# Attention and two feed-forward layers on one core: all products of round 0 with the values in the pair's second step, conversion work moved from the first step to the second

## The chip, the cores and the metric

The kernel runs on one NeuronCore of a Trainium2 chip. The metric is device time in microseconds (us), the median over runs. The engines are PE (TensorE, matrix products and transposes), DVE (VectorE), ACT (ScalarE), POOL (GpSimd) and SP (SyncE, which here issues DMAs). Each works through its own list of instructions in order and waits on semaphores of the others.

## The reference, cut to what matters

```python
scores = scale * np.matmul(q, k.transpose(0, 1, 3, 2))          # 4 x 8 heads, 576 x 576, head size 64
thresh = np.max(scores, axis=-1, keepdims=True) - tau
scores = np.where(scores >= thresh, scores, -1000000000.0)
attn = np.exp(scores - np.max(scores, axis=-1, keepdims=True))
attn = attn / (np.sum(attn, axis=-1, keepdims=True) + 1e-09)
attn_out = np.matmul(attn, v)
...
gate = 1.0 / (1.0 + np.exp(-(x @ w_gate)))                       # x: 2304 x 512, from attn_out
x = gate * (x @ w_val) @ w_out
h = x @ w_in
out = np.where(h >= 1, h, np.where(h <= -1, 0.0, (h + 1) ** 2 / 4)) @ w_out2
```

The change lies in the attention part alone. It alters the order of instructions and no arithmetic.

## The kernel before, in words

The 32 heads are worked as 16 pairs (`NP`), two heads of a pair side by side on the partitions. The 576 query rows of a pair are cut into five steps (`U = 5`): four of 128 rows for both heads, and a fifth that takes the remaining 64 rows of both heads together. The loop `for t in range(N + 9)` counts steps over all pairs, `N = 80`; step `u` of pair `p` is `t = 5 * p + u`. The text calls the steps of a pair first (`u = 0`) to fifth (`u = 4`). The pipeline is written out by hand in this loop: each engine gets its instructions in the order of the calls. In one step there stand, engine by engine:

- PE: `scores` (L252, in the fifth step L248) of this step into the PSUM tiles `wa` (first head) and `wb` (second head); `turns` (L295, L296), the transposes of the masked exponents of two steps ago, into `wt` and `left`; then `attend` (L319), the products with the values, for which the tables `rounds` and `final` say in which step they stand.
- DVE: `maxima` (L261) of this step, one instruction for `wa` and one for `wb`, each closed by a row DVE_READ_ACCUMULATOR that delivers the row's maximum; `masks` (L281) of the step before, one instruction for each head; last the background work.
- ACT: `copies` (L301, L305, L310, L311) of the transposes out of PSUM, `exponents` (L273), and `drain` (L329) of a finished sum `av`.
- POOL: the threshold (L264), a copy of the last 64 columns (L288), the scaling by the reciprocal sums (L350).

There is one `wa` and one `wb`. So `scores` of a step may write `wa` only when `maxima` of the step before has read it, and the same for `wb`; on PE these are two waits, on the first and on the second product of the step.

The products with the values of a pair go in two rounds. Round 0 covers the 256 query rows of the pair's first two steps, round 1 the other 320 rows. Each round is ten products: for both heads four blocks of 128 keys (`c` from 0 to 3) and the rest (`c = 4`, the tile `rl`), summed in the PSUM tile `av`. PE's fp32 products appear as two records each in the trace, so ten products are 20 records. Keys of `rounds` count from the pair's own first step: key 5 is the first step of the next pair, key 6 its second, and so on. Pair 15, the last, goes by `final`.

The background work (`background`, L155 to L169) prepares weights of the first feed-forward layer: one instruction on 128x512 elements at each `next(bg)`. It stands in three of the five steps of a pair, up to `t = 62`; afterwards the same places are "gaps" in which `ffn` puts splits of the attention output (L473, 128x768).

Of the kernel before, what the change touches and what calls it, by code (L numbers as in the profile page):

```python
# [29 lines left out]
def kernel(  # L30
# [169 lines left out]
    def attention():  # L200
# [23 lines left out]
        def load(p):  # L224
            t = qkp.tile([P, 2, S], F32, tag="qk", name="qk")
            nc.sync.dma_start(out=t[:, 0], in_=q[p])
            nc.sync.dma_start(out=t[:, 1], in_=k[p])
            qk[p] = t
# [9 lines left out]
        def corner(p):  # L238
            for e in range(2):
                es = slice(e * R, e * R + R)  # L240
                nc.gpsimd.tensor_copy(corners[p % 2][es, es], qk[p][es, 0, nf * P :])

        def scores(p, u):
            t = qk[p]
            for s in range(2):
                c = slice(s * HS, s * HS + HS)
                if u == nf:
                    nc.tensor.matmul(wa[:, s, :HS], corners[p % 2], t[:, 1, c], start=True, stop=True)  # L248
                    continue
                for e, w in enumerate((wa, wb)):  # L250
                    es = slice(e * D, e * D + D)
                    nc.tensor.matmul(  # L252
                        w[:, s, :HS], t[es, 0, u * P : u * P + P], t[es, 1, c], start=True, stop=True
                    )

        def maxima(p, u):

            t = sp.tile([P, 2, 2, HS], F32, tag="s", name="s")
            mx = mxs[(p * U + u) % 2]
            for e, w in enumerate((wa, wb)[: 1 if u == nf else 2]):  # L260
                nc.vector.tensor_scalar(  # L261
                    t[:, e], w[:, :, :HS], nscale, None, op0=ALU.mult, op1=ALU.min, accum_out=mx[:, 0, e : e + 1]
                )
                nc.gpsimd.tensor_scalar(  # L264
                    mx[:, 1, e : e + 1], mx[:, 0, e : e + 1], tau_b, None, op0=ALU.add
                )
            st[p, u] = t, mx

        def exponents(p, u):
            t, mx = st[p, u]  # L270
            ex = pe_.tile([P, 2, 2, HS], F32, tag="ex", name="ex")
            for e in range(1 if u == nf else 2):
                nc.scalar.activation(ex[:, e], t[:, e], AF.Exp, scale=-1.0, bias=mx[:, 0, e : e + 1])  # L273
            st[p, u] = t, mx, ex

        def masks(p, u):
            t, mx, ex = st.pop((p, u))
            pr = pt[p, u] = pp.tile([P, 2, S], F32, tag="p", name="p")
            for e in range(1 if u == nf else 2):
                c = 2 * nf if u == nf else e * nf + u  # L280
                nc.vector.scalar_tensor_tensor(  # L281
                    pr[:, e], t[:, e].rearrange("p a b -> p (a b)"), mx[:, 1, e : e + 1],
                    ex[:, e].rearrange("p a b -> p (a b)"), op0=ALU.is_le, op1=ALU.mult,
                    accum_out=sums[p % 2][:, c : c + 1],
                )
            lt = lts[p, u] = pp.tile([P, 2, R], F32, tag="lt", name="lt")
            x = pr[:, :, nf * P :] if u < nf else pr[:, :1, nf * P :].broadcast_to((P, 2, R))
            nc.gpsimd.tensor_copy(lt, x)  # L288

        def turns(p, u):  # L290
            pr = pt.pop((p, u))
            for e in range(1 if u == nf else 2):
                for c in range(nf):
                    cs = slice(c * P, c * P + P)
                    nc.tensor.transpose(wt[:, e, cs], pr[:, e, cs], ident)  # L295
            nc.tensor.transpose(left[:, :P], lts.pop((p, u)).rearrange("p a b -> p (a b)"), ident)  # L296

        def copies(p, u):
            r, o = min(u // 2, 1), u % 2 * P if u < nf else 2 * P
            if u < nf:  # L300
                nc.scalar.activation(  # L301
                    rt[r].rearrange("p e c n -> p (e c) n")[:, :, o : o + P],
                    wt.rearrange("p e (c n) -> p (e c) n", n=P), AF.Copy,
                )
                nc.scalar.activation(rl[r][:, o : o + P], left[:, :P], AF.Copy)  # L305
                return
            for e in range(2):
                es = slice(e * R, e * R + R)
                x = wt[:, 0].rearrange("p (c n) -> p c n", n=P)
                nc.scalar.activation(rt[r][:, e, :, o : o + R], x[:, :, es], AF.Copy)  # L310
                nc.scalar.activation(rl[r][es, o : o + R], left[es, es], AF.Copy)  # L311

        def attend(p, r, cs):


            n = NR[r]
            for c in cs:
                for e in range(2):
                    nc.tensor.matmul(  # L319
                        av[e * D : e * D + D, :n], vs[p % 3][:, e, c], rt[r][:, e, c] if c < nf else rl[r],  # L320
                        start=c == 0, stop=c == nf,
                    )
# [5 lines left out]
        def drain(p, r):  # L328
            nc.scalar.activation(x_of(p)[:, r * NR[0] : r * NR[0] + NR[r]], av[:, : NR[r]], AF.Copy)  # L329

        def denom(p):
            rs = sums[p % 2]
            nc.vector.reciprocal(rs, rs)

        def sum_rows(p):

            n = 2 * nf + 1
            nc.scalar.activation(rows[p % 2][:n], left[:n, P : 2 * P], AF.Copy)
            drs[p] = dram.tile([n, P], F32, tag="dr", name="dr")
            nc.sync.dma_start(out=drs[p], in_=rows[p % 2][:n])  # L340
# [7 lines left out]
        def normalise(p, s):  # L348
            x, c = x_of(p), slice(s * HS, s * HS + HS)
            nc.gpsimd.tensor_tensor(x[:, c], x[:, c], rbs[:, p % 2 * S :][:, c], op=ALU.mult)  # L350
# [28 lines left out]
        corner(0)  # L379
        bg = background()  # L380

        rounds = {5: (0, 0, 2), 6: (0, 2, 5), 7: (1, 0, 2), 8: (1, 2, 5)}
        final = {5: (0, 0, 5), 7: (1, 0, 5)}
        parts = {}
        for p in range(NP):
# [2 lines left out]
        for t in range(N + 9):  # L388
            p, u = divmod(t, U)
            on = t < N  # L390
            mk = divmod(t - 1, U) if 1 <= t <= N else None
            at = divmod(t - 2, U) if 2 <= t <= N + 1 else None

            pd, ud = divmod(t - U, U)
            pd2, ud2 = divmod(t - 2 * U, U)
            if ud2 in (2, 3) and 0 <= pd2 < NP:
                normalise(pd2, ud2 - 2)
            if on:
                scores(p, u)
            if t == N + 1:  # L400
                yield t - N, True
            if at:
                turns(*at)
            if ud == 2 and 0 <= pd < NP:
                nc.tensor.transpose(left[: 2 * nf + 1, P : 2 * P], sums[pd % 2], ident)
            for part in parts.get(t, ()):
                attend(*part)
            if on:
                maxima(p, u)
            if at:  # L410
                copies(*at)
            if on:
                exponents(p, u)
            if ud == 1 and 0 <= pd < NP:
                denom(pd)
            if ud == 2 and 0 <= pd < NP:
                sum_rows(pd)
            for part in parts.get(t, ()):
                if part[2][-1] == nf:
                    drain(*part[:2])  # L420
            if mk:
                masks(*mk)
                if mk[1] == nf:
                    nc.gpsimd.tensor_scalar(sums[mk[0] % 2], sums[mk[0] % 2], 1e-9, None, op0=ALU.add)
            if on and u in (0, 2, 3) and t > 2:
                if t <= 12 * U + 2:
                    next(bg, None)
                else:
                    yield t - N, "gap"
            if on:  # L430
                if u == 1 and p + 1 < NP:
                    corner(p + 1)
                if u == 2 and p + 2 < NP:
                    load(p + 2)
                if u == 4 and p + 2 < NP:
                    load_v(p + 2)
                if t == 1 or u == 2 and p % 2 == 0 and p < 12:
                    next(bg, None)
            if ud == 3 and 0 <= pd < NP:
                spread(pd)  # L440
            if t == N - 1:
                wides[:] = [wb, wa, wt]
            if t == N:
                run(bg)
                nc.scalar.activation(dummy, half, AF.Sigmoid)
                st1.close()
            if t == N + 2:
                st2.close()
                ps_o.close()
            yield t - N, False  # L450
# [497 lines left out]
```

## Time and profile before

| | |
|---|---|
| median of 3 runs | 1127.94 us (1127.83 to 1129.14) |
| the profiled execution, its own time | 1128.86 us |
| its span, first to last instruction | 1127.1 us |
| busy in the span | PE 1108.3, DVE 845.5, ACT 621.5, POOL 161.1 us |

Attention fills roughly the first 285 us of the span; the feed-forward layers the rest. Busy time of PE is modelled for pipelined products, so that it is the starts of its rows, and what stands between two of them, that carry an argument. A share of the whole span says little on a change in one stage: what counts there is which engine's instruction is late.

### The profile page before, as it was taken

Reading aid. Unit: us, or ns where it says so; the run is one execution under the profiler, and the core shown is the slowest. Engines: PE = TensorE matmul, PEld = TensorE weight load, DVE = VectorE, ACT = ScalarE, POOL = GpSimd, SP = SyncE. Lnnn points to the kernel's source line nnn. Section 1 sums busy time; section 2 is a strip of 40 time slices with the busy share of each in tenths; the row PEclk is TensorE's granted clock in tenths of the full one; section 3 lists DMA queues with packets and bytes.
Section 4 is the critical chain, followed back from the end, with each engine's and each line's share of the span. In section 5 each row is a group of like instructions: output and inputs, shape, how many; then the busy total and the mean of one; then the engine's idle time right before and its main releaser. Section 6 shows DMA issues by size and latency. Waiting matters only on the chain.

```text
span 1127.1 us, 17344 instructions
## 1 busy us (share of the span) xinstructions
PE 1108.3 (98%) x6372; PEld 946.5 (84%) x6372; DVE 845.5 (75%) x1484; ACT 621.5 (55%) x1048; POOL 161.1 (14%) x315
## 2 busy tenths in 40 slices
PE   8999999999899999999999999989999999999998
PEld 5666666666799999999999999979888888898887
DVE  6999999995899989776687663476767767776663
ACT  6787778886443435333344332365656665666553
POOL 3565666554100000000000000000000000000000
PEclk9999999999899999999999999989999999999999
DMA  4323322313466565555454443033321433243301
GB/s 132 90 77 85 103 87 62 85 52 127 162 203 205 169 213 198 187 167 174 174 184 153 159 153 109 1 112 112 113 106 63 168 113 112 68 156 114 113 19 57
DMA packets 65141, 139.09 MB, mean 123 GB/s; under 512 B 9616, under 2 KB 35872, under 8 KB 65056
## 3 DMA queue, kind: packets, MB, share of 16 engines
q1 hardware_dynamic: 64912, 137.98, 36.7%
q8 instruction: 50, 0.82, 0.3%
q14 instruction: 35, 0.29, 0.1%
q10 hardware_dynamic: 144, 0.00, 0.0%
HBM read 111.15 MB, written 26.81 MB: 122 GB/s over the span
## 4 chain that ended last, share of the span: by engine, by line
PE 91%; DVE 4%; ACT 2%; issue 1%; POOL 0%; DVEq 0%; POOLq 0%; ACTq 0%
PE y L739 15%; PE pu L606 14%; PE y L757 13%; PE pgv L482 8%; PE pgv L481 8%; PE pgv L483 8%; PE av L319 8%; PE w L252 7%; PE w L295 6%; PE w L248 2%; PE left L296 1%; ACT sqs L615 1%; ACT sqs L616 1%; ACT hh L624 1%; PE av L368 0%
## 5 line engine op out<-in xcount | busy, mean ns | idle before, releaser
L481 PE MATMUL pgv<-xflat,win 128*128 128x384 f32 x560 | 188.5, 337 | 5.6 <-ACT act L537 3.8
L739 PE MATMUL y<-wout,hh 128*128 128x512 f32 x576 | 186.0, 398 | 3.0 <-ACT hh L624 3.0
L482 PE MATMUL pgv<-xflat,win 128*128 128x384 f32 x560 | 188.3, 336 | 0.1
L483 PE MATMUL pgv<-xflat,win 128*128 128x384 f32 x560 | 188.2, 336 | 0.0
L757 PE MATMUL y<-hh,wout 128*128 128x512 f32 (+1 forms) x576 | 147.0, 337 | 0.0
L739 PEld LDWEIGHTS y<-wout,hh 128*128 128x128 f32 x576 | 109.4, 190 | 28.1 <-ACT hh L624 3.3
L261 DVE TENSOR_SCALAR_CACHE_REDUCE s<-w,nscale 128x576 f32<-128x576 f32 x144 | 112.7, 817 | 22.5 <-PE w L248 10.7
L541 DVE TENSOR_TENSOR act<-pgv,act 128x384 f32<-128x384 f32 x70 | 38.8, 555 | 105.0 <-PE pgv L483 104.6
L739 PE MATMUL y<-wout,hl 128*128 128x512 f32 x288 | 114.7, 398 | 0.2 <-DVE hl L625 0.2
L481 PEld LDWEIGHTS pgv<-xflat,win 128*128 128x128 f32 x560 | 105.8, 189 | 7.7 <-ACT act L537 4.1
L281 DVE SCALAR_TENSOR_TENSOR p<-s,mx,ex 128x576 f32<-128x576 f32 x144 | 111.7, 809 | 0.5 <-POOL lt L288 0.5
L537 ACT ACTIVATE act<-pgv 128x384 f32<-128x384 f32 x70 | 34.2, 489 | 137.4 <-PE pgv L483 137.2
L273 ACT ACTIVATE ex<-s,mx 128x576 f32<-128x576 f32 x144 | 104.8, 774 | 6.7 <-DVE s L261 6.4
L757 PEld LDWEIGHTS y<-hh,wout 128*128 128x128 f32 x576 | 98.4, 188 | 11.4
L264 POOL TENSOR_SCALAR mx<-mx,tau_b 128x1 f32<-128x1 f32 x144 | 98.1, 685 | 68.3 <-DVE s L261 68.2
L482 PEld LDWEIGHTS pgv<-xflat,win 128*128 128x128 f32 x560 | 106.0, 189 | 2.0 <-DVE xflat L473 0.4
L606 PE MATMUL pu<-xflat,win 128*128 128x384 f32 x576 | 105.1, 337 | 1.0 <-DVE sqs L685 0.7
L483 PEld LDWEIGHTS pgv<-xflat,win 128*128 128x128 f32 x560 | 105.9, 189 | 0.0
L542 ACT ACTIVATE hh<-act 128x384 fp32r<-128x384 f32 x72 | 38.0, 527 | 121.8 <-DVE act L541 121.3
L606 PEld LDWEIGHTS pu<-xflat,win 128*128 128x128 f32 x576 | 100.6, 188 | 2.4 <-DVE sqs L685 1.3
L757 PE MATMUL y<-hl,wout 128*128 128x512 f32 (+1 forms) x288 | 97.3, 338 | 0.0
L301 ACT ACTIVATE r<-w 128x1024 f32<-128x1024 f32 x64 | 65.7, 1026 | 47.7 <-PE w L295 47.7
(140 smaller groups left out, 1918.0 us busy)
## 6 DMA issues: line engine op xcount, KB each, us to landing
wmore<-saved SPq DMA_DIRECT2D x32, 512.0 KB
words<-in_moe_w_out_dram SPq DMA_DIRECT2D x26, 512.0 KB
tsum<-tsaved SPq DMA_DIRECT2D x24, 512.0 KB
wmore<-saved SPq DMA_DIRECT2D x15, 768.0 KB
words<-in_moe_w_in_dram SPq DMA_DIRECT2D x16, 512.0 KB
saved<-w SPq DMA_DIRECT2D x16, 512.0 KB
w<-saved SPq DMA_DIRECT2D x16, 512.0 KB
w<-saved SPq DMA_DIRECT2D x9, 768.0 KB
```

The lines of the kernel that those rows point to most:

```text
L252: nc.tensor.matmul(w[:, s, :HS], t[es, 0, u * P : u * P + P], t[es, 1, c], start=True, stop=True)
L261: nc.vector.tensor_scalar(t[:, e], w[:, :, :HS], nscale, None, op0=ALU.mult, op1=ALU.min, accum_out=mx[:, 0, e : e + 1])
L264: nc.gpsimd.tensor_scalar(mx[:, 1, e : e + 1], mx[:, 0, e : e + 1], tau_b, None, op0=ALU.add)
L273: nc.scalar.activation(ex[:, e], t[:, e], AF.Exp, scale=-1.0, bias=mx[:, 0, e : e + 1])
L281: nc.vector.scalar_tensor_tensor(pr[:, e], t[:, e].rearrange("p a b -> p (a b)"), mx[:, 1, e : e + 1], ex[:, e].rearrange("p a b -> p (a b ...
L319: nc.tensor.matmul(av[e * D : e * D + D, :n], vs[p % 3][:, e, c], rt[r][:, e, c] if c < nf else rl[r], start=c == 0, stop=c == nf,)
L481: nc.tensor.matmul(ps, ih[:, i, kk], xh[:, kk, c], start=(kk == 0), stop=False)
L482: nc.tensor.matmul(ps, ih[:, i, kk], xl[:, kk, c], start=False, stop=False)
L483: nc.tensor.matmul(ps, il[:, i, kk], xh[:, kk, c], start=False, stop=(kk == KD - 1))
L606: nc.tensor.matmul(ps[bank], l[:, k], r[:, k], start=bool(new) and k == m == 0, stop=k == HK - 1 and m == 2, skip_group_check=True,)
L739: nc.tensor.matmul(y[b], l[:, ts_], r, start=first and m == 0, stop=last and m == 2)
L757: nc.tensor.matmul(at(y, a, b), l[:, ds_], r[:, c], start=new and m == 0, stop=last and m == 2, skip_group_check=True,)
```

## The change

```diff
-        rounds = {5: (0, 0, 2), 6: (0, 2, 5), 7: (1, 0, 2), 8: (1, 2, 5)}
+        rounds = {6: (0, 0, 5), 7: (1, 0, 2), 8: (1, 2, 5)}
...
-            if on and u in (0, 2, 3) and t > 2:
+            if on and u in (1, 2, 3) and t > 2:
```

Before, round 0 had its key blocks 0 and 1 (four products) in the first step of the next pair and blocks 2 to 4 (six products) in the second. Now all ten stand in the second step. Round 1 is as before. The background instruction of the first step moves to the second; those of the third and fourth step stay. The instructions on ACT, POOL and SP stand in the same order as before.

PE in the first and second step of a pair, before: `w_126` is `wa`, `w_127` is `wb`, `w_128` is `wt`; the rows begin with the transposes of the first step.

```order
L295 MATMUL w_128<-ident,p 128x128 x8
L296 MATMUL left<-ident,lt 128x128
L319 MATMUL av<-r_160,v_166 64x256 x4
L252 MATMUL w_126<-qk 128x288
L252 MATMUL w_127<-qk 128x288
L252 MATMUL w_126<-qk 128x288
L252 MATMUL w_127<-qk 128x288
L295 MATMUL w_128<-ident,p 128x128 x4
L296 MATMUL left<-ident,lt 128x128
L319 MATMUL av<-r_160,v_166 64x256 x4
L319 MATMUL av<-rl_162,v_166 64x256 x2
L252 MATMUL w_126<-qk 128x288
```

The same place on PE now, from the same transposes on:

```order
L295 MATMUL w_128<-ident,p 128x128 x8
L296 MATMUL left<-ident,lt 128x128
L252 MATMUL w_126<-qk 128x288
L252 MATMUL w_127<-qk 128x288
L252 MATMUL w_126<-qk 128x288
L252 MATMUL w_127<-qk 128x288
L295 MATMUL w_128<-ident,p 128x128 x4
L296 MATMUL left<-ident,lt 128x128
L319 MATMUL av<-r_160,v_166 64x256 x8
L319 MATMUL av<-rl_162,v_166 64x256 x2
L252 MATMUL w_126<-qk 128x288
```

Four products have left the place between the first step's transposes and the second step's scores, and stand before the third step's scores.

DVE over the first and second step of a pair, before, from the first step's maxima on:

```order
L261 TENSOR_SCALAR s,mx_76<-w_126,nscale 128x576
L261 TENSOR_SCALAR s,mx_76<-w_127,nscale 128x576
L281 SCALAR_TENSOR_TENSOR p,sum_81<-s,mx_77,ex 128x576
L165 SCALAR_TENSOR_TENSOR high_84<-raw_87,high_84 128x512
L261 TENSOR_SCALAR s,mx_77<-w_126,nscale 128x576
L261 TENSOR_SCALAR s,mx_77<-w_127,nscale 128x576
L333 RECIPROCAL sum_81<-sum_81 128x9
L281 SCALAR_TENSOR_TENSOR p,sum_80<-s,mx_76,ex 128x576 x2
L261 TENSOR_SCALAR s,mx_76<-w_126,nscale 128x576
```

And now:

```order
L261 TENSOR_SCALAR s,mx_76<-w_126,nscale 128x576
L261 TENSOR_SCALAR s,mx_76<-w_127,nscale 128x576
L281 SCALAR_TENSOR_TENSOR p,sum_81<-s,mx_77,ex 128x576
L261 TENSOR_SCALAR s,mx_77<-w_126,nscale 128x576
L261 TENSOR_SCALAR s,mx_77<-w_127,nscale 128x576
L333 RECIPROCAL sum_81<-sum_81 128x9
L281 SCALAR_TENSOR_TENSOR p,sum_80<-s,mx_76,ex 128x576 x2
L165 SCALAR_TENSOR_TENSOR high_84<-raw_87,high_84 128x512
L261 TENSOR_SCALAR s,mx_76<-w_126,nscale 128x576
```

The conversion (here L165, at every other pair L157) has moved from behind the first step's masks to behind the second step's; both places come after the first step's maxima.

## Rows read from the trace of the kernel before

**Rows 1.** The page: its head, and PE's share from part 1.

```profile
span 1127.1 us, 17344 instructions
...
PE 1108.3 (98%) x6372; PEld 946.5 (84%) x6372; DVE 845.5 (75%) x1484; ACT 621.5 (55%) x1048; POOL 161.1 (14%) x315
```

**Rows 2.** Busy time by stretch: eleven pairs of attention, columns in the first line.

```profile
core 0: us, PE busy (x) PEld busy (x) DVE busy (x) ACT busy (x) POOL busy (x), PEclk, DMA share, GB/s
36.73:218.22 181.49, 181.49 (x1300) 115.24 (x1300) 167.19 (x440) 142.91 (x270) 110.83 (x209) 1.00 0.31 85
```

**Rows 3.** The chain that ended last: start, length, engine, tile, line, records.

```profile
102.72 1.18 PE w L252 x8
...
105.03 1.01 PE av L319 x8
...
107.92 1.45 PE av L319 x12
...
119.22 1.18 PE w L252 x8
...
270.22 2.31 PE av L319 x20
```

**Rows 4.** Timeline of DVE, fifth step to third: start, length, instruction [idle before].

```profile
101.78 0.82 DVE L261 TENSOR_SCALAR_CACHE_REDUCE s<-w,nscale 128x576 f32<-128x576 f32 x1 [0.69 <-PE w L248]
...
103.26 0.82 DVE L281 SCALAR_TENSOR_TENSOR p<-s,mx,ex 128x576 f32<-128x576 f32 x1
...
104.21 0.82 DVE L261 TENSOR_SCALAR_CACHE_REDUCE s<-w,nscale 128x576 f32<-128x576 f32 x1
...
104.95 0.81 DVE L261 TENSOR_SCALAR_CACHE_REDUCE s<-w,nscale 128x576 f32<-128x576 f32 x1
105.69 0.08 DVE L261 DVE_READ_ACCUMULATOR s<-w,nscale 128x1 f32 x1
...
106.43 0.69 DVE L165 SCALAR_TENSOR_TENSOR high<-raw,high 128x512 f32<-128x512 uint32 x1
107.25 0.82 DVE L261 TENSOR_SCALAR_CACHE_REDUCE s<-w,nscale 128x576 f32<-128x576 f32 x1
...
110.28 0.08 DVE L281 DVE_READ_ACCUMULATOR p<-s,mx,ex 128x1 f32 x1
110.56 0.82 DVE L261 TENSOR_SCALAR_CACHE_REDUCE s<-w,nscale 128x576 f32<-128x576 f32 x1 [0.20 <-PE w L252]
```

**Rows 5.** Timeline of PE over the end of the first step.

```profile
104.96 1.08 PE L319 MATMUL av<-r,v 128*64 128x256 f32 x8
105.98 1.24 PE L252 MATMUL w<-qk 64*128 64x288 f32 x8
```

**Rows 6.** Timeline of DVE and of PE's weight loads (PEld) at the start.

```profile
8.72 0.08 DVE L261 DVE_READ_ACCUMULATOR s<-w,nscale 128x1 f32 x1
...
8.85 0.78 PEld L252 LDWEIGHTS w<-qk 64*128 64x128 f32 x6 [0.44 <-DVE s L261]
...
11.14 0.08 DVE L261 DVE_READ_ACCUMULATOR s<-w,nscale 128x1 f32 x1
...
11.27 0.30 PEld L252 LDWEIGHTS w<-qk 64*128 64x128 f32 x4 [0.45 <-DVE s L261]
```

**Rows 7.** Groups of instructions by line: busy, mean ns; moved background work.

```profile
L165 DVE SCALAR_TENSOR_TENSOR high<-raw,high 128x512 f32<-128x512 uint32 x6 | 4.1, 687 | 0.0
...
L157 DVE TENSOR_SCALAR w<-high 128x512 uint32<-128x512 uint32 x6 | 2.5, 423 | 0.0
...
L473 DVE TENSOR_TENSOR xflat<-xall,xflat 128x768 fp32r<-128x768 f32 x4 | 3.8, 950 | 0.0
```

**Rows 8.** Busy time by stretch: the start, and around one fall of the clock.

```profile
0.00:20.00 20.00, 16.72 (x83) 11.56 (x83) 12.03 (x33) 10.35 (x16) 7.02 (x26) 1.00 0.57 185
...
745.00:753.57 8.57, 6.42 (x37) 6.09 (x35) 5.56 (x11) 3.02 (x7) 0.00 (x0) 1.00 0.43 174
753.57:760.39 6.82, 5.79 (x13) 4.22 (x14) 3.61 (x4) 5.73 (x7) 0.00 (x0) 0.50 0.01 2
```

## The prediction

> **What bounds the kernel now.** I read the page first: PE is busy for 98% of the span [rows 1], so the question is whether PE is the bound in the stage of the change too, or only on average. The table of stretches answers it: over eleven pairs of attention, 36.73 to 218.22 us, PE is busy for all 181.49 us, at the full granted clock; DVE comes next with 167.19 us, 92% [rows 2]. The chain of waits says the same: one pair runs from 102.72 to 119.22, 16.50 us, and every piece between is PE work [rows 3]. The view of waits has no wait of PE in that stretch.
>
> That PE waits for nobody does not mean that it is far from waiting. The timeline of DVE shows how far. In the first step of a pair DVE reads the two score tiles at 104.21 (wa) and 104.95 (wb), and the second reading is delivered by the row at 105.69 [rows 4]. PE starts the second step's scores, which overwrite those tiles, at 105.98 [rows 5]. What such a release takes is seen at the start of the kernel, where PE does wait for the same pair of instructions: delivery rows start at 8.72 and 11.14, the waiting weight loads at 8.85 and 11.27, 0.13 us later both times [rows 6]. So wb is free for PE at 105.69 + 0.13 = 105.82, and PE comes at 105.98: the slack is 0.16 us. It is hidden because just before it PE works on the four products that the change takes away, 104.96 to 105.98 [rows 5].
>
> Can DVE be earlier there? It stood idle 0.69 us before the fifth step's maxima at 101.78, and what ended that was PE, with the fifth step's scores (L248) [rows 4]. From there on its instructions follow each other at their own pace: the fifth step's one reading, two masks (the second at 103.26), then the two readings of the first step. So DVE's delivery is tied to PE's fifth-step scores. The reader is to see a loop: PE's fifth-step scores, DVE's five instructions, PE's second-step scores, and PE's work from there to the next fifth step.
>
> **The change part by part.** *Four products leave the first step.* PE's block there takes 1.01 us in the chain [rows 3], 1.02 us from start to start [rows 5]. Without it PE would come to the second step's scores at 104.96, 0.86 us before wb is free. The first products, on wa, may start at 104.95 + 0.13 = 105.08; those on wb wait until 105.82, and the rest of PE's list stands behind them. The start with 11.27 us shows what happens when wb comes later than wa: the later tile then takes its usual turn, and the step's end goes by it. So the second step's scores start, in effect, at 105.82 instead of 105.98: of 1.02 us removed, 0.16 is gained.
>
> *The four products join the six of the second step.* The six take 1.45 us, and ten in one block take 2.31 us, as seen after the loop, where the last pair's round 0 stands undivided [rows 3]. That adds 0.86 us in the second step, where PE has no idle time to put it in.
>
> As a sum of PE work alone the merger is a gain: 1.01 + 1.45 - 2.31 = 0.15 us a pair. The Trainium skill, TensorEngine Tiling (Array Packing), section Key Properties, says that changing the tiling mode drains TensorE. One block of 64-column products less means such changes less, and the 0.15 us agrees in sign. By that rule alone the change would be a gain of 0.15 us in each pair, which is the first rival's figure below.
>
> *The conversion leaves the first step.* It stands behind the first step's masks (L165 at 106.43) [rows 4], so it delays neither the readings at 104.21 and 104.95 nor the next fifth step. It buys PE nothing. What it frees, the second step's readings after 107.25, was not what PE waited for.
>
> *The conversion enters the second step.* It stands behind that step's masks and ahead of the third step's readings. Before, masks ended about 0.08 us after the row at 110.28, 3.11 us after the second step's readings began at 107.25; third-step readings began at 110.56, when PE's scores for them were there [rows 4]. Now second-step readings start no later than 107.25 - 0.16 = 107.09, masks end by 110.20, and a conversion of 0.687 us (L165) or 0.423 us (L157) ends by 110.89, in the three places after the conversions a split of 0.950 us (L473) by 111.15 [rows 7]. PE's third-step scores now come 0.86 - 0.16 = 0.70 us later, so the readings for them start at 111.26. All three fit. PE's own delay is the cover; without that delay only 0.20 us would be there [rows 4], and the conversion would be in the way.
>
> *What else moves.* ACT, POOL and SP keep their lists. Round 0's sum is ready later in the second step, and its copy out of PSUM has until round 1 begins in the third step. I cost it at nothing: there the third step's scores and transposes lie between, about 1.2 and 1.0 us by the like blocks of a pair (L252 at 102.72 takes 1.18) [rows 3]. From the third step to the fifth everything shifts as one, since PE sets each start there.
>
> *The sum.* Per pair +0.86 - 0.16 = +0.70 us. The place exists at the first step of pairs 1 to 15, so 15 times; the last pair's own rounds stand after the loop and are not touched. 15 x 0.70 = 10.5 us. The feed-forward layers begin that much later and are otherwise the same. Bounds for one pair: 0.86 - 0.29 = 0.57 if PE were released with no delay at 105.69, and 0.86 if the new wait on wb is no better than the old start; 15 times that is 8.6 to 12.9 us. I take 0.70, because the 0.13 us of the release was read twice on the very instructions. Against the profiled execution's 1128.86 us this gives 1139.4 us; the median of the three runs is 0.92 us lower, 1127.94, and the forecast is for a median: 1127.94 + 10.5 = 1138.5 us, 0.9% slower.
>
> **The rivals.** *Faster: the wait does not appear.* If DVE delivered wb by 104.96, only the merger's 0.15 us would be left, 15 x -0.15 = -2.2 us: 1125.7 us. For it: the four products and a DVE instruction leave the same step, and DVE idles 0.69 us two steps earlier [rows 4]. Against it: that idle time ends by PE's own scores, and the removed instruction stands behind the readings, not ahead. The delivery would have to come 0.73 us before 105.69; nothing in the order moves it. The other way to the same end would be that PE passes over the waiting scores and does other work. The waiting weight loads at 8.85 and 11.27 with 0.44 and 0.45 us idle [rows 6] show no sign of that. The Trainium skill, TensorE: Matmul & The Clock Gate, section The mechanism (of row and column tiling), says that only weight loads are pulled ahead and products stay in order; by that rule the wait stands, and the trace agrees.
>
> *No change: half the wait counts.* If the products on wa, released at 105.08, did useful work while those on wb wait, so that the step ended as if begun at about 105.1, the gain would be 0.88 and the loss 0.86: 1127.6 us. Against it: both heads' products run side by side, so doing one early shortens nothing.
>
> *Slower still: DVE becomes the bound in the second step.* If the cover of the moved conversions failed, they would add up to 6 x 0.687 + 6 x 0.423 + 3 x 0.950 = 9.5 us [rows 7]: up to 1148.0 us. It decides if the second step's chain on DVE grows by more than the 0.11 us (with L473) or 0.37 us (with L165) left above; for the former that is little, so a part of it, 3 x 0.3 us, is quite possible and in my range.
>
> *Slower still: the clock falls.* After 745.00 to 753.57, with PE busy for 6.42 of 8.57 us, the clock was granted at 0.50 (1.2 GHz) for 6.82 us [rows 8], which costs 3.4 us of PE time. Once would give 1141.9 us, once in every pair 15 x 3.4 = 51 us more, 1189.6. Against it: the new wait idles PE for about 0.86 us in 17.2, and the first 20 us, with PE busy for 16.72, ran at 1.00 [rows 8]. The Trainium skill, TensorE: Matmul & The Clock Gate, section A second HAM failure mode, tells of a kernel whose short idle moments between groups of products set the clock swinging; by that the dearer case would hold, and no row of this trace's attention shows it.
>
> **How the numbers follow.** The new wait as computed: 0.88. Faster, no wait: 0.03. No change: 0.03. DVE bound: 0.04. Clock: 0.02. The forecast is that of the first, 1138.5. Its own range is 8.6 to 12.9 us on 1127.94, that is 1136.5 to 1140.8. To it I add some 1.2 us to either side for what runs differ by (the three span 1.3 us) and for part of the L473 case: 1135.3 to 1142.0. A measurement of this kernel tells about 0.2%, 2.3 us, from no change: faster 0.03, same 0.03, slower 0.94.
>
> **What would show it.** In the changed kernel PE should wait about 0.8 us for DVE's L261 at the second step's scores (L252), 15 times, some 12 us in all in the view of waits, and nowhere else in attention. One pair should last 17.2 us instead of 16.50. The block of 20 L319 records should take 2.3 us in each second step. DVE should wait for PE before the third step's readings for some tenths of a us. The feed-forward part should be as long as before. The forecast is wrong if pairs last 16.35 us (no wait), if DVE has no idle time left before the third step's readings (DVE bound), or if the granted clock in attention is below 1.00.

## The result and the profile after

The changed kernel takes 1138.68 us (median, 1137.69 to 1139.84), against 1127.88 us for the kernel before in the same comparison: the ratio is 1.0094, 95% interval 1.0082 to 1.0107. That is 0.9% slower; the forecast was 1138.5 us. The profiled execution took 1139.84 us, its span is 1138.1 us, 11.0 us more than before [rows 1].

Nearly all of it lies in attention. Cut at the start of the last pair's round 0, which is the row `PE av L319 x20` in the chain of both kernels (270.22 us before, 281.01 us after), the table of stretches has for the rest, first of before, then of after (length of the stretch, then busy time of PE, PEld, DVE, ACT and POOL):

```profile
270.22:1127.10 856.88, 842.51 (x4511) 776.66 (x4510) 602.89 (x849) 412.01 (x658) 5.47 (x6) 0.99 0.40 137
```

```profile
281.01:1138.10 857.09, 842.63 (x4510) 776.57 (x4510) 602.98 (x849) 411.85 (x658) 4.69 (x6) 0.99 0.39 136
```

The feed-forward part is as long as it was, within 0.21 us; the part ahead of it is 10.79 us longer.

The chain of waits of after, over one pair (start, length, what):

```profile
104.56 1.18 PE w L248 x4
...
108.94 0.10 DVE s L261
109.08 1.97 PE w L252 x8
...
111.75 2.31 PE av L319 x20
...
121.76 1.18 PE w L248 x4
```

From one fifth step to the next it is 121.76 - 104.56 = 17.20 us; before it was 16.50 us a pair [rows 3]. DVE has entered a chain that was PE alone, just ahead of the second step's scores. The timeline of DVE shows why (it answers to [rows 4]):

```profile
105.76 0.82 DVE L261 TENSOR_SCALAR_CACHE_REDUCE s<-w,nscale 128x576 f32<-128x576 f32 x1 [0.69 <-PE w L248]
...
108.19 0.82 DVE L261 TENSOR_SCALAR_CACHE_REDUCE s<-w,nscale 128x576 f32<-128x576 f32 x1
108.94 0.08 DVE L261 DVE_READ_ACCUMULATOR s<-w,nscale 128x1 f32 x1
...
109.68 0.08 DVE L261 DVE_READ_ACCUMULATOR s<-w,nscale 128x1 f32 x1
...
110.63 0.82 DVE L261 TENSOR_SCALAR_CACHE_REDUCE s<-w,nscale 128x576 f32<-128x576 f32 x1
...
113.66 0.68 DVE L165 SCALAR_TENSOR_TENSOR high<-raw,high 128x512 f32<-128x512 uint32 x1
115.26 0.82 DVE L261 TENSOR_SCALAR_CACHE_REDUCE s<-w,nscale 128x576 f32<-128x576 f32 x1 [0.92 <-PE w L252]
```

And the timeline of PE over the same two steps (it answers to [rows 5]):

```profile
106.64 1.24 PE L252 MATMUL w<-qk 64*128 64x288 f32 x8
107.82 1.09 PE L295 MATMUL w<-ident,p 128*128 128x128 f32 x8
...
109.08 1.97 PE L252 MATMUL w<-qk 64*128 64x288 f32 x8
110.98 0.66 PE L295 MATMUL w<-ident,p 128*128 128x128 f32 x4
...
111.67 1.95 PE L319 MATMUL av<-r,v 128*64 128x256 f32 x16
...
113.98 1.24 PE L252 MATMUL w<-qk 64*128 64x288 f32 x8
```

Before, PE's first-step scores, second-step transposes and third-step scores stood here:

```profile
102.66 1.24 PE L252 MATMUL w<-qk 64*128 64x288 f32 x8
...
107.15 0.66 PE L295 MATMUL w<-ident,p 128*128 128x128 f32 x4
...
109.29 1.24 PE L252 MATMUL w<-qk 64*128 64x288 f32 x8
```

From the fifth step's reading to the second delivery DVE needs 109.68 - 105.76 = 3.92 us; before it needed 105.69 - 101.78 = 3.91 us [rows 4]. DVE is not slower. PE comes earlier and cannot use it: scores on `wa` begin at 109.08, 0.14 us after the first delivery, and the eight records now spread over 1.97 us, where they took 1.24 us, because all but the first product on `wa` begin 0.74 us later, behind the second delivery. The transposes then follow at 110.98, and the block of twenty pushes the third step's scores to 113.98.

One thing to see in reading: the wait is not where one looks for waits. The table of stretches still has PE busy for 188.87 of 189.50 us over eleven pairs:

```profile
37.50:227.00 189.50, 188.87 (x1302) 119.42 (x1300) 167.36 (x442) 142.83 (x269) 101.76 (x209) 1.00 0.29 81
```

The view of waits for PE, 20 to 290 us, has 1.3 us in all, and the kernel before has the same two rows there:

```profile
PE w L295 <- ACT r L301: 1.0, 1, 1.0
PE w L252 <- DVE s L261: 0.3, 1, 0.3
```

The groups by line show where it went. L252 over eleven pairs, before and after (count, busy us, mean ns, idle before):

```profile
L252 PE MATMUL w<-qk 64*128 64x288 f32 x354 | 55.1, 429 | 0.0
```

```profile
L252 PE MATMUL w<-qk 64*128 64x288 f32 x352 | 62.6, 432 | 0.6
```

But for two records the number is the same, and one lasts about as long as before, yet the group is busy for 7.5 us more, 0.68 us a pair. PE's weight loads for the second step's scores, and PE itself in the first part of the wait, show why:

```profile
109.08 0.29 PEld L252 LDWEIGHTS w<-qk 64*128 64x128 f32 x2 [0.30 <-DVE s L261]
109.81 0.78 PEld L252 LDWEIGHTS w<-qk 64*128 64x128 f32 x6 [0.44 <-DVE s L261]
```

```profile
109.08 0.75 PE L252 MATMUL w<-qk 64*128 64x288 f32 x2
```

Loads start 0.14 and 0.13 us behind the two deliveries. The first two belong to the first of the step's four products, on `wa`. The next product in PE's list is on `wb`, and the other one on `wa` stands behind it; so three of the four start after the second delivery. The records of the first product last 0.75 us, as long as the wait for `wb`, so that PE as a whole counts as idle for only 0.6 us in eleven pairs. The kernel before shows the same picture at its start, where deliveries came at 7.98 and 8.72: eight records over 1.97 us, with no idle time inside, and a reading that begins soon after the second release.

```profile
8.11 1.97 PE L252 MATMUL w<-qk 64*128 64x288 f32 x8 [0.92 <-DVE s L261]
```

```profile
9.66 0.82 DVE L261 TENSOR_SCALAR_CACHE_REDUCE s<-w,nscale 128x576 f32<-128x576 f32 x1 [0.86 <-PE w L252]
```

The Trainium skill, Trainium Kernel Development and Optimization, section Performance Expectations, warns that busy time of products is a bad measure of how close a kernel is to its best possible rate, because they are pipelined. That it misleads, this trace shows too: PE's share of the span is 98% in both kernels, though one is 11.0 us longer. The reason seen here is another one: the first product on `wa` runs while `wb` is awaited.

### The profile page after: what moved, and what is told of

Same layout as the page of the kernel before. It is cut to its first block, busy times and chain, and to the rows that moved or that the text cites. A ratio compares the mean times of both kernels' runs of the same rounds, so it can differ in the third digit from the quotient of the medians.

```text
span 1138.1 us, 17344 instructions
## 1 busy us (share of the span) xinstructions
PE 1118.3 (98%) x6372; PEld 952.1 (84%) x6372; DVE 845.7 (74%) x1484; ACT 621.2 (55%) x1048; POOL 150.7 (13%) x315
## 4 chain that ended last, share of the span: by engine, by line
PE 87%; DVE 7%; issue 3%; ACT 2%; DVEq 0%; POOL 0%; POOLq 0%; ACTq 0%
PE y L739 15%; PE pu L606 14%; PE y L757 13%; PE pgv L482 8%; PE pgv L483 8%; PE pgv L481 8%; PE av L319 7%; PE w L252 6%; PE w L295 4%; DVE p L281 2%; PE w L248 2%; DVE s L261 1%; ACT sqs L615 1%; ACT sqs L616 1%; ACT hh L624 1%
## 5 line engine op out<-in xcount | busy, mean ns | idle before, releaser
L252 PE MATMUL w<-qk 64*128 64x288 f32 x512 | 93.1, 434 | 2.6 <-DVE s L261 1.6
```

The lines of the kernel that those rows point to most:

```text
L252: nc.tensor.matmul(w[:, s, :HS], t[es, 0, u * P : u * P + P], t[es, 1, c], start=True, stop=True)
```

## The experiments

Each experiment was timed against runs of the kernel before on the same chip: a median of 1128.66 us beside the two runs with six and with all ten products in the first step, 1128.73 us beside the other four. The theory is that PE's second-step scores wait for DVE's reading of the second tile, and that only the four moved products cause it. The rivals are that the moved conversion costs time, and that number or length of the blocks does.

**Products only.**

```diff
-        rounds = {5: (0, 0, 2), 6: (0, 2, 5), 7: (1, 0, 2), 8: (1, 2, 5)}
+        rounds = {6: (0, 0, 5), 7: (1, 0, 2), 8: (1, 2, 5)}
```

> All ten products in the second step, the conversion left in the first. Theory (PE's second-step scores wait for DVE's reading of the second score tile): the conversion stands behind that reading in either place, so all of the loss stays: 15 x 0.70 = 10.5 us, 1138.5 us. Rival (the conversion in the second step makes DVE late for the third step): with the conversion back the loss goes or shrinks by up to 9.5 us, 1127.9 to 1133 us.

Measured: 1139.43 us, ratio 1.0094 (1.0081 to 1.0108), the same as the whole change. So the moved products carry the loss, and putting the conversion back gives nothing back. In the trace it even costs a little: the two pairs with the split L473 in that place take 17.51 us here (the blocks of twenty start at 214.32, 231.83 and 249.34) against 17.21 in the changed kernel, and those with L165 17.25. That is 2 x 0.30 + 6 x 0.04 = 0.8 us, less than the times can tell apart; what causes it was not followed up.

**Conversion only.**

```diff
-            if on and u in (0, 2, 3) and t > 2:
+            if on and u in (1, 2, 3) and t > 2:
```

> Products as before, the conversion alone moved to the second step. Theory: DVE is late for the third step's readings by 0.22 us (L157) or 0.49 us (L165), but PE's scores behind them have 0.75 us to spare, so 0 to 0.1 us a pair: 1127.9 to 1129.4 us. Rival (the conversion is the cost): the full 0.42 and 0.69 us in 12 pairs and 0.95 in three, up to 1137.4 us.

Measured: 1128.33 us, ratio 1.0001 (0.9992 to 1.0010): no difference. DVE is indeed late for the third step's readings, and PE has enough in hand. DVE, then PE:

```profile
109.96 0.68 DVE L165 SCALAR_TENSOR_TENSOR high<-raw,high 128x512 f32<-128x512 uint32 x1
110.56 0.81 DVE L261 TENSOR_SCALAR_CACHE_REDUCE s<-w,nscale 128x576 f32<-128x576 f32 x1
...
112.03 0.08 DVE L261 DVE_READ_ACCUMULATOR s<-w,nscale 128x1 f32 x1
```

```profile
108.96 1.24 PE L252 MATMUL w<-qk 64*128 64x288 f32 x8
...
112.61 1.24 PE L252 MATMUL w<-qk 64*128 64x288 f32 x8
```

Readings begin 1.60 us after the third step's scores here, where it was 1.27 us before (109.29 to 110.56). With the 0.13 us of the release, the delivery at 112.03 lets PE go on at 112.16; PE comes at 112.61 and has 0.45 us in hand. Only the two pairs with the longer L473 in that place lose by it: in the chain a block of their round 1 follows the last one after 16.94 us (230.91 to 247.85), before after 16.65 (230.95 to 247.60), 0.6 us in all, which the times do not show.

**Two products in the first step.**

```diff
-        rounds = {5: (0, 0, 2), 6: (0, 2, 5), 7: (1, 0, 2), 8: (1, 2, 5)}
+        rounds = {5: (0, 0, 1), 6: (0, 1, 5), 7: (1, 0, 2), 8: (1, 2, 5)}
```

> Two of round 0's ten products in the first step (key block 0), eight in the second; conversion as before. Theory: two products are 0.43 us of PE work. PE would come 0.27 us before the second tile is free, so of 0.43 us taken away only 0.16 is gained: +0.27 us a pair, 4.1 us, 1132.0 us. Rival (the number of blocks or changes of tiling mode decides): there are two blocks as before, so no change, 1127.9 us.

Measured: 1133.35 us, ratio 1.0049 (1.0036 to 1.0062), 4.6 us between the medians. The count of blocks is unchanged and the time is not, so the rival falls. Two pairs in the chain last 33.59 us, 16.79 us each, 0.29 us over before:

```profile
75.72 1.88 PE av L319 x16
...
109.31 1.88 PE av L319 x16
```

**Six products in the first step.**

```diff
-        rounds = {5: (0, 0, 2), 6: (0, 2, 5), 7: (1, 0, 2), 8: (1, 2, 5)}
+        rounds = {5: (0, 0, 3), 6: (0, 3, 5), 7: (1, 0, 2), 8: (1, 2, 5)}
```

> Six of round 0's ten products in the first step (key blocks 0 to 2), four in the second; conversion as before. Theory: the second step's scores start 0.43 us later, so do their readings and the delivery behind them: 108.73 + 0.43 = 109.16, free for PE at 109.29, where PE with 0.43 us less work in the second step comes at 109.29 too. No change beyond 0.05 us a pair: 0 to 0.8 us slower than before. Rival (fewer products in the first step cost, more gain): the reverse of two products in the first step, some 4 us faster.

Measured: 1129.20 us, ratio 1.0003 (0.9994 to 1.0012). Here the slack of the third step's scores is used up to the last hundredth: the second delivery, and PE's start 0.13 us behind it.

```profile
109.73 0.08 DVE L261 DVE_READ_ACCUMULATOR s<-w,nscale 128x1 f32 x1
```

```profile
109.86 1.24 PE L252 MATMUL w<-qk 64*128 64x288 f32 x8
```

**All ten in the first step.**

```diff
-        rounds = {5: (0, 0, 2), 6: (0, 2, 5), 7: (1, 0, 2), 8: (1, 2, 5)}
+        rounds = {5: (0, 0, 5), 7: (1, 0, 2), 8: (1, 2, 5)}
```

> All ten products of round 0 in the first step, none in the second; conversion as before. Theory: one block as in the changed kernel, but now the third step's scores lose their cover. Scores of the second step start at 104.96 + 2.31 = 107.27, their readings at 108.54, the second delivery at 110.02, PE is released at 110.15 where it came at 109.29 before: +0.86 us a pair, 12.9 us slower than before. Rival (the merged block is worth 0.15 us a pair and only the second step's scores were in danger): 2.2 us faster than before.

Measured: 1143.18 us, ratio 1.0114 (1.0098 to 1.0130), 12.9 us by the ratio and 14.5 us between the medians. The same single block as in the changed kernel, and the loss is at the other end: the third step's scores have lost their cover and wait for the second step's two deliveries, at 114.01 and 114.74. Those on `wa` start at 114.14, the others behind the second delivery, and the eight records spread over 1.97 us again.

```profile
114.01 0.08 DVE L261 DVE_READ_ACCUMULATOR s<-w,nscale 128x1 f32 x1
...
114.74 0.08 DVE L261 DVE_READ_ACCUMULATOR s<-w,nscale 128x1 f32 x1
```

```profile
111.99 1.24 PE L252 MATMUL w<-qk 64*128 64x288 f32 x8
113.16 0.66 PE L295 MATMUL w<-ident,p 128*128 128x128 f32 x4
...
114.14 1.97 PE L252 MATMUL w<-qk 64*128 64x288 f32 x8 [0.21 <-DVE s L261]
```

Two of its blocks of twenty stand 17.36 us apart, 0.86 us over before:

```profile
92.39 2.31 PE av L319 x20
109.75 2.31 PE av L319 x20
```

**The conversion in the fifth step**, with the products of the changed kernel (the edit is against that kernel).

```diff
-            if on and u in (1, 2, 3) and t > 2:
+            if on and u in (2, 3, 4) and t > 2:
```

> As the changed kernel, but the conversion stands in the fifth step, behind its masks and ahead of the first step's readings, in place of the second step. Theory: there it lies on the path to the second tile's release; without it the readings begin 0.21 us after the last delivery row, with it 0.42 or 0.69 us after, so 6 x 0.21 + 6 x 0.48 = 4.1 us more than the changed kernel: 1142.7 us (1146.5 at most, if the full durations count). Rival (DVE's load counts, not the place): the same instructions in number, 1138.6 us.

Measured: 1142.10 us, ratio 1.0117 (1.0102 to 1.0133), some 2.6 us more than the changed kernel's ratio gives. DVE has as many conversions, and the place makes them dear, so the place counts and not DVE's load. The size was expected at 4.1 us, too much, and the timeline of DVE shows the reason:

```profile
108.84 0.69 DVE L165 SCALAR_TENSOR_TENSOR high<-raw,high 128x512 f32<-128x512 uint32 x1
109.45 0.81 DVE L261 TENSOR_SCALAR_CACHE_REDUCE s<-w,nscale 128x576 f32<-128x576 f32 x1
...
126.44 0.42 DVE L157 TENSOR_SCALAR w<-high 128x512 uint32<-128x512 uint32 x1
126.78 0.81 DVE L261 TENSOR_SCALAR_CACHE_REDUCE s<-w,nscale 128x576 f32<-128x576 f32 x1
```

The reading behind the conversion starts 0.61 or 0.34 us after it, not 0.69 or 0.42. Less the 0.21 us that stand there without it, that is 0.40 and 0.13 us, 6 x 0.53 = 3.2 us. The chain agrees: with the conversion in that place pairs last 17.33 us (L157; blocks of twenty at 112.99 and 130.32) and 17.60 us (L165; 95.39 and 112.99), against 17.21 in the changed kernel.

## Why the prediction was right

- *The bound and the loop.* It named PE as bound, with 0.16 us of slack at one place. Five places of the same ten products bear it out: with 0, 2, 4, 6 and 10 of them in the first step the loss is 0.70, 0.29, 0 (before), 0 and 0.86 us a pair.
- *Removed products gain 0.16 us.* The second step's transposes come 107.15 - 102.66 = 4.49 us after the first-step scores before, and 110.98 - 106.64 = 4.34 us after them now. So 0.15 us is gained.
- *Added products cost 0.86 us.* From the second step's transposes to the third step's scores: 113.98 - 110.98 = 3.00 us, against 109.29 - 107.15 = 2.14 us before. That is the 0.86 us of the forecast.
- *The sum.* 15 x 0.70 = 10.5 us was forecast; 10.79 us stands in the trace ahead of the last pair's round 0, and 10.8 us between the medians. That these come so close is in part chance: 0.44 us of the 10.79 is there at the first fifth step, ahead of everything that was moved (PE's L248 starts at 16.88 before and 17.32 now). The fifteen pairs themselves are 10.35 us longer. Two of them lost 0.56 and not 0.70 us: with L473 in the first step they took 16.65 us before, not 16.50. The forecast counted three places with L473; the trace has two.
- *The conversion costs nothing.* Right, but its working was off. With the products moved, DVE is idle for 0.92 us ahead of the third step's readings, where the forecast had left only 0.37 us. It let the second step's readings begin 1.27 us after the scores. They begin at 110.63, 0.82 us after the loads of 109.81, because one of the first head's two products has run by then; at the start of the kernel before it was 9.66 - 8.85 = 0.81 us. So the cover was larger than worked out, and the rival on L473 never came into play. That the conversion's leaving the first step buys nothing was off by the 0.8 us named under the first experiment.
- *Wrong: where the wait would show.* The forecast let PE stand idle while `wb` is awaited, some 12 us in the view of waits. That view has nothing of it; its 0.3 us stands in the kernel before too. The wait is there, as busy time of L252, and 8.11 to 10.08 us of the trace before could have told so.
- *The rivals.* Faster fell: the delivery did not move. No change fell: the early product on `wa` lets DVE read sooner, but PE's transposes come 110.98 - 109.81 = 1.17 us after the second loads, as they came 107.15 - 105.98 = 1.17 us after the scores before. A fall of the clock did not come: the granted clock over eleven pairs is 1.00, as before.

No version here beats the kernel before. The places tried for round 0 lose on both sides of four to six products in the first step. That the merger of two blocks is worth 0.15 us of PE work is only argued from block lengths; every version with one block had a wait that swallowed it.

## What to carry to other kernels

An engine that is busy all the time can still have a second engine 0.16 us behind it. Before work is moved out from between two dependent steps, take the other engine's delivery and compare it with the moment at which the first engine would come; what lies beyond is lost, and the moved work is paid for at its new place, here with 0.86 us. Work that keeps an engine busy while a buffer is read is a cover with a measurable length: here 0.86 of its 1.02 us.

## What the runs showed of the hardware that was not expected

When two products that run side by side wait for two tiles, and one tile comes 0.74 us later, the trace here counts the whole stretch as busy PE: 1.97 us for eight records in place of 1.24 us. The weight loads show the wait, as two groups, each 0.13 or 0.14 us behind a delivery. On DVE the row after a 128x512 conversion starts up to 0.08 us before that row's end (0.61 us after the start of one that lasts 0.69), so that durations added up overstate a chain; starts must be subtracted.
